# A reordered instruction list for a linear-attention and feed-forward kernel: a lead for each run of small matmuls in the planner's costs

## The chip, the cores and the metric

The kernel runs on one core of a Trainium2 chip. The metric is device time in microseconds. "PE" is TensorE's matmul stream and "PEld" its weight loads, "DVE" is VectorE, "ACT" ScalarE, "POOL" GpSimd, "SP" the engine that issues the DMAs.

## The reference

Four batches of four heads have 1088 positions of 32 dimensions. Queries and keys go through a feature map of 64 products, then linear attention, then a feed-forward layer with a gate over all 4352 tokens:

```python
def phi(x):                        # r = 8
    a = einsum('rd,bhsd->bhsr', S1, x)
    b = einsum('rd,bhsd->bhsr', S2, x)
    return einsum('bhsi,bhsj->bhsij', a, b).reshape(..., 64)
kv  = einsum('bhsf,bhsd->bhfd', phi(k), v)
z   = sum(phi(k), axis=2)
x   = einsum('bhsf,bhfd->bhsd', phi(q), kv) / (einsum('bhsf,bhf->bhs', phi(q), z) + 1e-6)
h   = x @ w_in                     # (4352, 128) @ (128, 2048)
g   = h * clip(h + 3, 0, 6) / 6
out = g @ w_out                    # (4352, 2048) @ (2048, 128)
```

## The kernel before

The tokens are cut into eight chunks of 512 and a last one of 256 that holds what is left over of each batch. A step of the feed-forward part is one chunk and one pair of 128-wide blocks of the hidden layer: six matmuls make h in PSUM (high and low parts of x and w_in, lines 811, 812 and 817), ACT takes relu (825), DVE the gate (828), ACT the high part gh (832), DVE or POOL the low part gl (836), and six matmuls add into o (857, 858 with gh, 860 with gl). There are 8.5 chunks x 8 pairs x 12 = 816 such matmuls of 512 columns, some of them cut into halves of 256.

Ahead of that stand the small operations of the attention part. "ab" projects keys or queries on S1 and S2 (530, and 535 for chunks 2 on, the "far" form), ACT or DVE copies it (539, 543), DVE or POOL makes the products (558), "kv" adds a tile of 128 keys into a batch's PSUM bank (593; ACT copies the finished bank to SBUF at 618), "tr" and "xt" are transposes (713, 664), and "nd" gives numerator and denominator for two tiles of queries (636), which DVE divides (643 to 647). For chunks 2 on, features and x are turned by DVE and through DRAM instead (745, 773, 751, 756, 778, 782). The weights are split into high and low parts in nine passes on ACT and DVE (371 to 396). Loads start at line 423; the first thirteen are chained by a one-element copy on POOL (428), so that one starts after the fourth one before it has landed. Up to 17 us in the plan PE runs a filler matmul (354) where nothing else is ready.

Every engine works through its instructions in the order in which they were emitted, and that order is the plan's. `Plan.order` plays the program through with a cost for each operation: at each point in time it walks the operations whose inputs and buffers are there, least due first, and gives each to an idle engine. The dues come from the constants at the top: STEP between feed-forward steps, DUES for the four stages after h, LAG for o, LEADS for the small operations (a lead is taken off the due; the first set is for batch 0 and chunk 0, the second for the other batches and the far chunks, the third for chunk 1), W_DUE and CONV_LEAD for the weights. gl, the products and some others may go on DVE or POOL; `choose` decides. PSUM has two buffers of two banks for h, two banks "o" and two banks "a" for the small operations; SBUF has 5 buffers for g and 4 each for gh and gl.

Of the kernel before, what the change touches and what calls it, by code (L numbers as in the profile page):

```python
# [23 lines left out]
HP = P // 2  # L24
Q = P // 4
# [24 lines left out]
NEAR = 2  # L50
# [46 lines left out]
SPLIT = 2  # L97


STEP = 5.06  # L100
DUES = (317.92, 316.34, 129.31, 384.08)
LAG = 128.57
W_DUE = (-152.92, 321.22, 23.24, 201.42, 251.62, 14.82, 266.57, 276.24)
CONV_LEAD = (-252.29, -232.94, 463.37, -221.73, 549.89, 31.5, 265.14, 219.73, 219.47)
LOAD_DUE = {}
LEADS = ({'ab': -466.98, 'cp': -244.73, 'ph': 113.36, 'kv': -102.29, 'kvb': -199.83, 'tr': -78.56, 'trcp': -30.35, 'nd': -572.11, 'norm': 297.56, 'xt': 543.02, 'xh': -868.0, 'xl': 204.57, 'k0': -407.3, 'kld': 146.8, 'vld': -256.29, 'qld': -79.85, 'rd': -154.99, 'xw': 402.82, 'xr': 513.46}, {'ab': 106.42, 'cp': 408.81, 'ph': 46.58, 'kv': 85.72, 'kvb': -43.81, 'tr': -441.07, 'trcp': -288.36, 'nd': -2.3, 'norm': -121.67, 'xt': 347.83, 'xh': 86.64, 'xl': 378.1, 'k0': 9.14, 'kld': 371.66, 'vld': 59.77, 'qld': 218.44, 'rd': 139.58, 'xw': 405.77, 'xr': 51.94}, {'ab': -161.26, 'cp': -355.61, 'ph': 225.14, 'kv': -82.13, 'kvb': 258.9, 'tr': -84.99, 'trcp': -282.18, 'nd': 9.09, 'norm': 441.52, 'xt': -380.46, 'xh': -96.54, 'xl': -168.68, 'k0': 149.54, 'kld': -6.91, 'vld': 496.37, 'qld': 447.25, 'rd': -88.95, 'xw': -359.0, 'xr': 167.27})


HOLD = 10.14
HOLD_DUE = -34.33  # L110
SOON = 0.51
SOON_DUE = 27.65
PATIENCE = 0.0


@dataclass(eq=False)
class Op:

# [15 lines left out]
    dual: bool = False  # L134
    moved: float = 0.0
    recs: int = 0


@dataclass(eq=False)
# [9 lines left out]
class Plan:  # L149
# [2 lines left out]
    def __init__(self):  # L152
        self.ops = []

    def add(self, cost, due, deps, emit, bufs=(), cols=0, ready=0.0, moved=0.0, dual=False, recs=0):
        deps = [d for d in deps if d is not None]
        op = Op(cost, due, emit, list(bufs), cols, len(deps), ready, dual=dual, moved=moved, recs=recs)
        for d in deps:
            d.then.append(op)
        for b in op.bufs:  # L160
            b.left += 1
        self.ops.append(op)
        return op

    def fetched(self, t, recs):

        self.begun += recs
        need = self.begun - HELD
        if need > 0:
            t = max(t, self.asked[(need - 1) // MORE] + FETCH)  # L170
        while self.begun >= ASK + MORE * len(self.asked):
            self.asked.append(t)
        return t

    def speed(self, tick):

# [40 lines left out]
    def order(self):  # L217
        self.cols = {}
        self.port = 0.0
        self.begun, self.asked = 0, []  # L220
        self.moving = MOVING
        free, at = dict(BUFS), dict(START)
        free["o"] -= 1
        avail = sorted((o for o in self.ops if not o.waits), key=lambda o: o.due)
        out, ends, wakes, t, left = [], [], [FILL_UNTIL, *at.values()], 0.0, len(self.ops)
        heapify(wakes)
        n_out = 0
        while left:
            t = heappop(wakes)
            while wakes and wakes[0] <= t + 1e-6:  # L230
                t = heappop(wakes)
            t += 1e-7
# [12 lines left out]
            began = []  # L245
            for op in avail:
                if op.ready > t or not all(b.held or any(free[g] for g in b.tags) for b in op.bufs):
                    continue
                e = self.choose(op, t, at, soon)
                if e is None:  # L250
                    continue
                if e == PE and t < FILL_UNTIL and self.short(t, op.cost[PE], op.cols):
                    break
                for b in op.bufs:
                    if not b.held:
                        b.held = True
                        b.tag = next(g for g in b.tags if free[g])
                        free[b.tag] -= 1
                op.engine, op.start = e, t
                op.end = at[e] = self.run(self.fetched(t, op.recs), op.cost[e], op.cols) if e == PE else t + op.cost[e]  # L260
                if e == DVE and op.dual:
                    self.port = op.end
                if e == SP:
                    self.moving = max(self.moving, op.end - ISSUE + BEGUN) + op.moved / RATE
                    op.lat = self.moving + LANDED - op.end
                began.append(op)
            for op in began:
                avail.remove(op)
                n_out += 1
                left -= 1  # L270
                heappush(ends, (op.end + op.lat + FREED, n_out, op))
                heappush(wakes, op.end)
                heappush(wakes, op.end + op.lat + FREED)
                for o in op.then:
                    same = len(o.cost) == 1 and op.engine in o.cost
                    o.ready = max(o.ready, op.end + op.lat + (LATENCY[op.engine] if not same or op.lat else 0.13 if op.engine == DVE else 0.0))
                    o.waits -= 1
                    if not o.waits:
                        insort(avail, o, key=lambda x: x.due)
                        heappush(wakes, o.ready)  # L280
# [45 lines left out]
def fused_kernel(ctx: ExitStack, tc: tile.TileContext, qT, kT, v1, sb, w_in, w_out, outT):  # L326
# [18 lines left out]
    kvb = []  # L345
# [171 lines left out]
    def features(src, n, name, tag, due, ld, srcb, psb, eng_cost, LEAD, far=False, w=HP):  # L517
# [40 lines left out]
            engines[e].tensor_tensor(out, a_, b_, op=ALU.mult)  # L558

        if far:  # L560
            o1 = plan.add({PE: 0.1 + 0.121 * n}, due - LEAD["ab"], [ld], mm_far, [srcb, pb, abb], 256 * n, S_READY, recs=8)
            o2 = plan.add({DVE: 0.12 + 0.067 * n}, due - LEAD["cp"], [o1], cp_far, [pb, abb])
        else:
            o1 = plan.add({PE: 0.13 + 0.115 * n if w == HP else 0.137 + 0.112 * n}, due - LEAD["ab"], [ld], mm, [srcb, pb, abb], 256 * n, S_READY, recs=8 * n if w == HP else 16 * n)
            o2 = plan.add({ACT: 0.06 + 0.0535 * n}, due - LEAD["cp"], [o1], cp, [pb, abb])
        parts = []
        for t0 in range(0, n, SPLIT):
# [9 lines left out]
    def keys(b, due, psbs, ph_eng):  # L577
# [25 lines left out]
        for half in range(2):  # L603
            t0, n = KGROUPS[2 * b + half]
            g = 2 * b + half
            d = due - (LEAD["k0"] if half == 0 else 0)
            lk, kb, kbox = load_keys(g, d - LEAD["kld"])
            lv, vb, vbox = load_values(g, d - LEAD["vld"])
            T, o3, phb = features(kbox, n, f"k{g}", "kph", d, lk, kb, psbs[half], ph_eng[half], LEAD, w=KEY_COLS[b])
            for t in range(n):  # L610
                i = t0 + t - b * KT
                prev = plan.add({PE: 0.175 if KV_COLS[b] == Q else 0.26}, d - LEAD["kv"] + 0.3 * t, [o3[t], lv, prev], partial(kv, t=t, i=i, T=T, vbox=vbox), [phb, vb, kvbuf], 528, recs=32 if KV_COLS[b] == Q else 16)

        def halves(_):
            for e in (0, F):
# [8 lines left out]
    def divided(c, due, T, t, m, ready, phTb, nb, xb, LEAD):  # L624
# [22 lines left out]
            nc.vector.tensor_tensor(x, nd[:, :, 0:D], rden.broadcast_to([P, 4 * m, D]), op=ALU.mult)  # L647

        batches = range(batch_of(c0), batch_of(c0 + n - 1) + 1)
        a = plan.add({PE: 0.1 + 0.26 * m if c < NEAR else 0.11 + 0.245 * m}, due - LEAD["nd"] - lag, [ready, *(o for b in batches for o in kv_done[b])], nd, [phTb, nb, xb], 528 * m, recs=16 * m if c < NEAR else 32 * m)  # L650
        return plan.add({DVE: 0.56 + 0.1 * m}, due - LEAD["norm"] - lag, [a], norm, [nb, xb])

    def turn_x(c, due, T, norms, xb, xpb, LEAD):
# [292 lines left out]
```

## Time and profile before

| what | value |
|---|---|
| median of 3 runs | 246.84 us (245.31 to 247.11) |
| profiled execution, its own time | 244.85 us |
| span of that execution | 243.0 us |
| PE, DVE, ACT, POOL busy | 96%, 76%, 68%, 63% |

The span runs from the first to the last instruction of the profiled execution; 1.85 us of its own time lie around it. Starts in the rows are microseconds from the start of the span. PE's recorded matmuls overlap one another, so the time that one takes is read from start to start.

### The profile page before, as it was taken

Reading aid. Unit: us, or ns where it says so; the run is one execution under the profiler, and the core shown is the slowest. Engines: PE = TensorE matmul, PEld = TensorE weight load, DVE = VectorE, ACT = ScalarE, POOL = GpSimd, SP = SyncE. Lnnn points to the kernel's source line nnn. Section 1 sums busy time; section 2 is a strip of 40 time slices with the busy share of each in tenths; the row PEclk is TensorE's granted clock in tenths of the full one; section 3 lists DMA queues with packets and bytes.
Section 4 is the critical chain, followed back from the end, with each engine's and each line's share of the span. In section 5 each row is a group of like instructions: output and inputs, shape, how many; then the busy total and the mean of one; then the engine's idle time right before and its main releaser. Section 6 shows DMA issues by size and latency. Waiting matters only on the chain.

```text
span 243.0 us, 5464 instructions
## 1 busy us (share of the span) xinstructions
PE 233.8 (96%) x2214; PEld 182.2 (75%) x2214; DVE 184.7 (76%) x246; ACT 164.5 (68%) x205; POOL 154.1 (63%) x102
## 2 busy tenths in 40 slices
PE   8969789999999999999999899999999999999994
PEld 3757666787777778877878687777888878888894
DVE  2869999999899899788657756857648883747643
ACT  3455476888697648756766866849857875878571
POOL 2742867999699998474879844035663305867441
PEclk9999999999999999999999999999999999999999
DMA  6889973032037559704423000000100010001010
GB/s 206 263 282 386 373 249 115 1 88 87 4 87 184 180 146 295 239 0 136 127 89 86 18 29 20 25 0 3 43 0 0 0 43 3 0 0 46 0 43 22
DMA packets 18007, 23.80 MB, mean 98 GB/s; under 512 B 1728, under 2 KB 11072, under 8 KB 17984
## 3 DMA queue, kind: packets, MB, share of 16 engines
q1 hardware_dynamic: 17984, 23.48, 30.5%
q8 instruction: 17, 0.28, 0.5%
q14 instruction: 6, 0.05, 0.1%
HBM read 16.26 MB, written 7.21 MB: 97 GB/s over the span
## 4 chain that ended last, share of the span: by engine, by line
PE 86%; POOL 5%; issue 2%; DMA 2%; ACT 2%; DVE 1%; POOLq 0%; ACTq 0%
PE h L811 13%; PE o L857 13%; PE o L860 13%; PE h L817 12%; PE h L812 12%; PE o L858 12%; PE nd L636 3%; DMA woraw<-w_out_dram 2%; POOL gl L836 2%; PE warm L354 2%; PE kvps L593 2%; POOL ph_k L558 2%; PE abps_k L530 2%; PE abps_q L535 1%; PE xps L664 1%
## 5 line engine op out<-in xcount | busy, mean ns | idle before, releaser
L836 POOL TENSOR_TENSOR gl<-g,gh 128x1024 fp32r<-128x1024 f32 (+1 forms) x50 | 117.9, 2368 | 63.0 <-ACT gh L832 36.9
L828 DVE SCALAR_TENSOR_TENSOR g<-g,h 128x1024 f32<-128x1024 f32 (+1 forms) x72 | 82.9, 1156 | 24.7 <-ACT g L825 24.1
L825 ACT ACTIVATE g<-h 128x1024 f32<-128x1024 f32 (+1 forms) x72 | 70.3, 979 | 40.7 <-POOL gl L836 20.9
L832 ACT CAST gh<-g 128x1024 fp32r<-128x1024 f32 (+1 forms) x72 | 71.5, 1001 | 15.0 <-PE o L858 10.6
L811 PE MATMUL h<-xh,wi_hi 128*128 128x512 f32 (+1 forms) x148 | 56.8, 384 | 0.9 <-DVE g L828 0.9
L817 PE MATMUL h<-xl,wi_hi 128*128 128x512 f32 (+1 forms) x148 | 56.0, 378 | 0.0
L812 PE MATMUL h<-xh,wi_lo 128*128 128x512 f32 (+1 forms) x148 | 55.7, 376 | 0.0
L857 PE MATMUL o<-gh,wo_hi 128*128 128x512 f32 (+1 forms) x144 | 55.6, 389 | 0.0
L858 PE MATMUL o<-gh,wo_lo 128*128 128x512 f32 (+1 forms) x144 | 54.6, 382 | 0.0
L860 PE MATMUL o<-gl,wo_hi 128*128 128x512 f32 (+1 forms) x144 | 43.4, 385 | 0.0
L836 DVE TENSOR_TENSOR gl<-g,gh 128x1024 fp32r<-128x1024 f32 (+1 forms) x22 | 31.6, 1438 | 14.6 <-PE o L860 8.5
L811 PEld LDWEIGHTS h<-xh,wi_hi 128*128 128x128 f32 x148 | 27.7, 187 | 8.5 <-DVE g L828 1.3
L817 PEld LDWEIGHTS h<-xl,wi_hi 128*128 128x128 f32 x148 | 27.7, 187 | 5.9
L857 PEld LDWEIGHTS o<-gh,wo_hi 128*128 128x128 f32 x144 | 27.0, 188 | 6.7 <-issue 0.6
L812 PEld LDWEIGHTS h<-xh,wi_lo 128*128 128x128 f32 x148 | 27.8, 188 | 5.2
L858 PEld LDWEIGHTS o<-gh,wo_lo 128*128 128x128 f32 x144 | 27.0, 188 | 5.4
L860 PEld LDWEIGHTS o<-gl,wo_hi 128*128 128x128 f32 x144 | 25.8, 188 | 5.7 <-issue 0.4
L558 POOL TENSOR_TENSOR ph_k<-ab_k 128x512 f32<-128x512 f32 (+1 forms) x14 | 13.4, 978 | 10.9 <-ACT ab_k L539 10.9
L558 POOL TENSOR_TENSOR ph_q<-ab_q 128x512 f32<-128x512 f32 x15 | 15.8, 1073 | 0.9 <-ACT ab_q L539 0.5
L636 PEld LDWEIGHTS nd<-kvb,phT 128*32 128x32 f32 (+1 forms) x480 | 8.6, 113 | 4.0 <-issue 3.3
L593 PEld LDWEIGHTS kvps<-v,ph_k 128*32 128x32 f32 (+3 forms) x504 | 7.3, 113 | 5.4 <-issue 3.4
L593 PE MATMUL kvps<-v,ph_k 128*32 128x33 f32 (+3 forms) x504 | 8.8, 202 | 2.1 <-issue 1.6
(77 smaller groups left out, 165.8 us busy)
## 6 DMA issues: line engine op xcount, KB each, us to landing
phd<-pht SPq DMA_DIRECT2D x24, 128.0 KB, 3.9
phT<-phd SPq DMA_DIRECT2D x6, 512.0 KB, 4.4
wiraw<-w_in_dram SPq DMA_DIRECT2D x4, 512.0 KB, 5.5
qT<-qT_dram SPq DMA_DIRECT2D x8, 256.0 KB, 5.5
woraw<-w_out_dram SPq DMA_DIRECT2D x4, 512.0 KB, 5.4
outT_dram<-os SPq DMA_DIRECT2D x8, 256.0 KB, 2.0
xd<-xt SPq DMA_DIRECT2D x24, 64.0 KB, 1.8
xT<-xd SPq DMA_DIRECT2D x6, 256.0 KB, 2.7
```

Of the source, the lines that this page charges most:

```text
L558: engines[e].tensor_tensor(out, a_, b_, op=ALU.mult)
L593: nc.tensor.matmul(K["ps"][e : e + k, w], T["ph"][:rows, t, h * F + f : h * F + f + k], vbox[0][:rows, t, w], start=i == 0 and h < 2, stop ...
L811: nc.tensor.matmul(T["h"][:, u, i:j_], wi_hi[:, f], x, start=True, stop=False)
L812: nc.tensor.matmul(T["h"][:, u, i:j_], wi_lo[:, f], x, start=False, stop=False)
L817: nc.tensor.matmul(T["h"][:, u, i:j_], wi_hi[:, f], x, start=False, stop=True)
L825: nc.scalar.activation(T["g"][:, :, :n], T["h"][:, :, :n], AF.Relu, bias=3.0, scale=1.0)
L828: nc.vector.scalar_tensor_tensor(T["g"][:, :, :n], T["g"][:, :, :n], 6.0, T["h"][:, :, :n], op0=ALU.min, op1=ALU.mult)
L832: nc.scalar.copy(T["gh"][:, :, :n], T["g"][:, :, :n])
L836: engines[e].tensor_tensor(T["gl"][:, :, :n], T["g"][:, :, :n], T["gh"][:, :, :n].bitcast(F32), op=ALU.subtract)
L857: nc.tensor.matmul(o, wo_hi[:, f], T["gh"][:, u, :n], start=first and u == 0, stop=False)
L858: nc.tensor.matmul(o, wo_lo[:, f], T["gh"][:, u, :n], start=False, stop=False)
L860: nc.tensor.matmul(o, wo_hi[:, f], T["gl"][:, u, :n], start=False, stop=last and u == 1)
```

## The change

Two things change. First, the cost of a small operation on PE is split in two: a cost for itself, and a lead that the plan adds when the operation just before it on PE was of another kind. Kinds are "ab", "far", "kv" and "nd"; all other operations have no kind and no lead, and they end a run. The cost of an operation that stands alone stays within 0.03 us of what it was, but for kv in the batch-0 form (0.26 to 0.36 us) and in the other form (0.175 to 0.26 us). What the operations emit is untouched.

Second, all constants that set the order have new values. In LEADS, the second set has for example nd from -2.3 to -47.89, kld from 371.66 to 610.73 and qld from 218.44 to 355.87. `choose` itself is as before, so its rule for gl and the products is changed through SOON, SOON_DUE and PATIENCE alone, and its rule for holding an engine free through HOLD and HOLD_DUE.

```diff
-STEP = 5.06
-DUES = (317.92, 316.34, 129.31, 384.08)
-LAG = 128.57
-W_DUE = (-152.92, 321.22, 23.24, 201.42, 251.62, 14.82, 266.57, 276.24)
-CONV_LEAD = (-252.29, -232.94, 463.37, -221.73, 549.89, 31.5, 265.14, 219.73, 219.47)
+STEP = 4.31
+DUES = (334.45, 304.68, 247.67, 421.33)
+LAG = 116.65
+W_DUE = (-66.68, 326.64, -31.04, 253.22, 362.18, -253.11, 299.63, 339.63)
+CONV_LEAD = (-304.42, -129.34, 469.79, -119.14, 763.88, 26.11, 358.72, 292.57, 281.21)
...
-HOLD = 10.14
-HOLD_DUE = -34.33
-SOON = 0.51
-SOON_DUE = 27.65
-PATIENCE = 0.0
+HOLD = 33.3
+HOLD_DUE = -86.68
+SOON = 6.01
+SOON_DUE = -49.92
+PATIENCE = 0.93
...
+    def taken(self, op):
+
+        cost = op.cost[PE] + (op.lead if op.kind != self.last else 0.0)
+        self.last = op.kind
+        return cost
...
-                op.end = at[e] = self.run(self.fetched(t, op.recs), op.cost[e], op.cols) if e == PE else t + op.cost[e]
+                op.end = at[e] = self.run(self.fetched(t, op.recs), self.taken(op), op.cols) if e == PE else t + op.cost[e]
...
                 op = Op({PE: 0.214}, 0.0, self.filler, [], 512, start=t, engine=PE, recs=2)
+                self.last = ""
...
-            o1 = plan.add({PE: 0.1 + 0.121 * n}, due - LEAD["ab"], [ld], mm_far, [srcb, pb, abb], 256 * n, S_READY, recs=8)
+            o1 = plan.add({PE: 0.107 * n}, due - LEAD["ab"], [ld], mm_far, [srcb, pb, abb], 256 * n, S_READY, recs=8, lead=0.156, kind="far")
...
-            o1 = plan.add({PE: 0.13 + 0.115 * n if w == HP else 0.137 + 0.112 * n}, due - LEAD["ab"], [ld], mm, [srcb, pb, abb], 256 * n, S_READY, recs=8 * n if w == HP else 16 * n)
+            o1 = plan.add({PE: 0.115 * n if w == HP else 0.112 * n}, due - LEAD["ab"], [ld], mm, [srcb, pb, abb], 256 * n, S_READY, recs=8 * n if w == HP else 16 * n, lead=0.135, kind="ab")
...
-                prev = plan.add({PE: 0.175 if KV_COLS[b] == Q else 0.26}, d - LEAD["kv"] + 0.3 * t, [o3[t], lv, prev], partial(kv, t=t, i=i, T=T, vbox=vbox), [phb, vb, kvbuf], 528, recs=32 if KV_COLS[b] == Q else 16)
+                prev = plan.add({PE: 0.15 if KV_COLS[b] == Q else 0.25}, d - LEAD["kv"] + 0.3 * t, [o3[t], lv, prev], partial(kv, t=t, i=i, T=T, vbox=vbox), [phb, vb, kvbuf], 528, recs=32 if KV_COLS[b] == Q else 16, lead=0.11, kind="kv")
...
-        a = plan.add({PE: 0.1 + 0.26 * m if c < NEAR else 0.11 + 0.245 * m}, due - LEAD["nd"] - lag, [ready, *(o for b in batches for o in kv_done[b])], nd, [phTb, nb, xb], 528 * m, recs=16 * m if c < NEAR else 32 * m)
+        a = plan.add({PE: 0.25 * m if c < NEAR else 0.233 * m}, due - LEAD["nd"] - lag, [ready, *(o for b in batches for o in kv_done[b])], nd, [phTb, nb, xb], 528 * m, recs=16 * m if c < NEAR else 32 * m, lead=0.135, kind="nd")
```

## Rows read from the trace of the kernel before

**Rows 1.** The page of the profile: the span, and the busy time of PE and DVE.

```profile
span 243.0 us, 5464 instructions
...
PE 233.8 (96%) x2214; PEld 182.2 (75%) x2214; DVE 184.7 (76%) x246; ACT 164.5 (68%) x205; POOL 154.1 (63%) x102
```

**Rows 2.** The view of the span by stretches: length, busy time of each engine (instructions), granted clock, DMA share, GB/s. The first six rows cut the span at the events told in the text, the last one is the stretch from 40 to 80 us.

```profile
0.00:5.55 5.55, 4.78 (x11) 1.46 (x11) 1.25 (x7) 1.93 (x4) 1.49 (x11) 1.00 0.59 190
5.55:33.40 27.85, 23.51 (x623) 18.52 (x622) 23.84 (x47) 13.83 (x29) 15.03 (x23) 1.00 0.92 322
33.40:134.85 101.45, 101.45 (x1060) 77.27 (x1060) 88.81 (x130) 73.79 (x87) 85.78 (x46) 1.00 0.41 118
134.85:135.75 0.90, 0.05 (x2) 0.01 (x1) 0.84 (x1) 0.90 (x2) 0.88 (x1) 1.00 0.00 0
135.75:239.81 104.06, 104.06 (x522) 84.96 (x522) 69.98 (x63) 73.69 (x84) 50.95 (x23) 1.00 0.04 16
239.81:243.00 3.19, 0.00 (x1) 0.00 (x0) 0.00 (x0) 0.38 (x1) 0.00 (x0) 0.85 0.12 41
...
40.00:80.00 40.00, 40.00 (x434) 30.28 (x433) 38.87 (x56) 31.68 (x39) 36.65 (x21) 1.00 0.33 88
```

**Rows 3.** PE in order of time, a stretch of feed-forward steps without a small operation (48 matmuls from the first row to the second).

```profile
46.94 0.40 PE L857 MATMUL o<-gh,wo_hi 128*128 128x512 f32 x1
...
58.14 0.40 PE L811 MATMUL h<-xh,wi_hi 128*128 128x512 f32 x1
```

**Rows 4.** PE in order of time around visits to small operations: the last big matmul before, the small ones, and the first two big ones after.

```profile
59.31 0.40 PE L817 MATMUL h<-xl,wi_hi 128*128 128x512 f32 x1
...
59.64 0.77 PE L593 MATMUL kvps<-v,ph_k 128*32 128x33 f32 x64
...
60.33 0.50 PE L857 MATMUL o<-gh,wo_hi 128*128 128x512 f32 x1
...
60.67 0.39 PE L858 MATMUL o<-gh,wo_lo 128*128 128x512 f32 x1
...
61.46 0.67 PE L636 MATMUL nd<-kvb,phT 128*32 128x66 f32 x32
...
62.06 0.50 PE L860 MATMUL o<-gl,wo_hi 128*128 128x512 f32 x1
...
82.09 1.13 PE L636 MATMUL nd<-kvb,phT 128*32 128x66 f32 x64
83.16 0.50 PE L857 MATMUL o<-gh,wo_hi 128*128 128x512 f32 x1
...
33.40 0.33 PE L593 MATMUL kvps<-v,ph_k 128*32 128x33 f32 x16
33.73 0.47 PE L811 MATMUL h<-xh,wi_hi 128*128 128x512 f32 x1
```

**Rows 5.** PE in order of time: the first and the last visit to small operations after 33.73 us (19 in all), and the last nd run of the far chunks (10 runs for 13 operations; the first is the one at 61.46 us in Rows 4).

```profile
35.30 0.89 PE L593 MATMUL kvps<-v,ph_k 128*32 128x33 f32 x64
...
168.69 0.67 PE L636 MATMUL nd<-kvb,phT 128*32 128x66 f32 x32
...
171.72 0.38 PE L664 MATMUL xps<-ident,x 128*128 128x128 f32 x2
```

**Rows 6.** PE in order of time in the ramp: where it stood idle, with the idle time and its releaser in brackets, and the first and the last of the five fillers there (x2 is two).

```profile
6.59 0.39 PE L354 MATMUL warm<-const-bfloat16-1.0 128*128 128x512 bf16 x1
...
15.18 0.65 PE L530 MATMUL abps_k<-s_ab,kT 128*32 128x64 f32 x32 [1.80 <-ACT mag_wo L371]
...
17.34 0.60 PE L354 MATMUL warm<-const-bfloat16-1.0 128*128 128x512 bf16 x2
...
24.99 0.76 PE L593 MATMUL kvps<-v,ph_k 128*32 128x33 f32 x64 [0.42 <-POOL ph_k L558]
...
27.40 0.25 PE L593 MATMUL kvps<-v,ph_k 64*32 64x33 f32 x4 [0.82 <-issue]
...
32.29 0.45 PE L593 MATMUL kvps<-v,ph_k 128*32 128x33 f32 x29 [0.74 <-issue]
```

**Rows 7.** ACT and POOL in order of time around that first hole.

```profile
14.44 0.66 ACT L371 ACTIVATE mag_wo<-woraw 128x512 f32<-128x512 f32 x1 [2.03 <-DMA woraw<-w_out_dram]
15.00 0.42 ACT L618 COPY kvb<-kvps 64x66 f32<-64x66 f32 x2
...
15.17 0.18 POOL L428 COPY qT<-kT 128x1 f32<-128x1 f32 x1 [0.45 <-DMA kT<-kT_dram]
```

**Rows 8.** The one hole of PE after the ramp, and POOL before it.

```profile
127.61 8.12 POOL L836 TENSOR_TENSOR gl<-g,gh 128x1024 fp32r<-128x1024 f32 x3
...
135.75 0.50 PE L811 MATMUL h<-xh,wi_hi 128*128 128x512 f32 x1 [0.85 <-DVE g L828]
```

**Rows 9.** The groups of gl on the page: where it ran, its duration, and what POOL idled for.

```profile
L836 POOL TENSOR_TENSOR gl<-g,gh 128x1024 fp32r<-128x1024 f32 (+1 forms) x50 | 117.9, 2368 | 63.0 <-ACT gh L832 36.9
...
L836 DVE TENSOR_TENSOR gl<-g,gh 128x1024 fp32r<-128x1024 f32 (+1 forms) x22 | 31.6, 1438 | 14.6 <-PE o L860 8.5
```

**Rows 10.** gl alone on DVE and POOL from 40 to 80 us: busy time (instructions).

```profile
40.00:80.00 40.00, 0.00 (x0) 26.27 (x11) 1.00 0.33 88
```

**Rows 11.** The end of the span: the last matmuls, the last copy.

```profile
239.42 0.39 PE L860 MATMUL o<-gl,wo_hi 128*128 128x256 f32 x2
...
239.85 0.38 ACT L876 ACTIVATE os<-o 128x256 f32<-128x256 f32 x1 [2.40 <-PE o L860]
```

More of the change, by code (lines that the diff above doesn't have):

```diff
@@ L97 @@
 SPLIT = 2
-STEP = 5.06
-DUES = (317.92, 316.34, 129.31, 384.08)
-LAG = 128.57
-W_DUE = (-152.92, 321.22, 23.24, 201.42, 251.62, 14.82, 266.57, 276.24)
-CONV_LEAD = (-252.29, -232.94, 463.37, -221.73, 549.89, 31.5, 265.14, 219.73, 219.47)
-LOAD_DUE = {}
-LEADS = ({'ab': -466.98, 'cp': -244.73, 'ph': 113.36, 'kv': -102.29, 'kvb': -199.83, 'tr': -78.56, 'trcp': -30.35, 'nd': -572.11, 'norm': 297.56, 'xt': 543.02, 'xh': -868.0, 'xl': 204.57, 'k0': -407.3, 'kld': 146.8, 'vld': -256.29, 'qld': -79.85, 'rd': -154.99, 'xw': 402.82, 'xr': 513.46}, {'ab': 106.42, 'cp': 408.81, 'ph': 46.58, 'kv': 85.72, 'kvb': -43.81, 'tr': -441.07, 'trcp': -288.36, 'nd': -2.3, 'norm': -121.67, 'xt': 347.83, 'xh': 86.64, 'xl': 378.1, 'k0': 9.14, 'kld': 371.66, 'vld': 59.77, 'qld': 218.44, 'rd': 139.58, 'xw': 405.77, 'xr': 51.94}, {'ab': -161.26, 'cp': -355.61, 'ph': 225.14, 'kv': -82.13, 'kvb': 258.9, 'tr': -84.99, 'trcp': -282.18, 'nd': 9.09, 'norm': 441.52, 'xt': -380.46, 'xh': -96.54, 'xl': -168.68, 'k0': 149.54, 'kld': -6.91, 'vld': 496.37, 'qld': 447.25, 'rd': -88.95, 'xw': -359.0, 'xr': 167.27})
-HOLD = 10.14
-HOLD_DUE = -34.33
-SOON = 0.51
-SOON_DUE = 27.65
-PATIENCE = 0.0
+STEP = 4.31
[3 more added lines that the diff above has]
+CONV_LEAD = (-304.42, -129.34, 469.79, -119.14, 763.88, 26.11, 358.72, 292.57, 281.21)
+LOAD_DUE = {}
+LEADS = ({'ab': -412.15, 'cp': -326.18, 'ph': 97.12, 'kv': 2.11, 'kvb': -467.32, 'tr': 2.94, 'trcp': -199.99, 'nd': -493.05, 'norm': 300.27, 'xt': 562.42, 'xh': -826.62, 'xl': 273.94, 'k0': -388.4, 'kld': 185.32, 'vld': -260.13, 'qld': 153.85, 'rd': -347.91, 'xw': 515.91, 'xr': 488.45}, {'ab': 101.81, 'cp': 447.08, 'ph': -75.15, 'kv': 72.05, 'kvb': 108.18, 'tr': -403.05, 'trcp': -266.36, 'nd': -47.89, 'norm': -170.28, 'xt': 328.11, 'xh': -122.6, 'xl': 393.0, 'k0': 24.53, 'kld': 610.73, 'vld': -71.26, 'qld': 355.87, 'rd': 29.1, 'xw': 220.04, 'xr': 54.17}, {'ab': -116.77, 'cp': -474.19, 'ph': 283.03, 'kv': -24.83, 'kvb': 337.37, 'tr': -48.73, 'trcp': -260.0, 'nd': 5.34, 'norm': 345.01, 'xt': -503.62, 'xh': -321.35, 'xl': -246.99, 'k0': 30.86, 'kld': -194.6, 'vld': 436.55, 'qld': 598.55, 'rd': -94.74, 'xw': -529.34, 'xr': 129.65})
+HOLD = 33.3
[3 more added lines that the diff above has]
+PATIENCE = 0.93
 @dataclass(eq=False)
@@ L136 @@
     recs: int = 0
+    lead: float = 0.0
+    kind: str = ""
 @dataclass(eq=False)
@@ L153, in __init__, with add @@
         self.ops = []
-    def add(self, cost, due, deps, emit, bufs=(), cols=0, ready=0.0, moved=0.0, dual=False, recs=0):
+    def add(self, cost, due, deps, emit, bufs=(), cols=0, ready=0.0, moved=0.0, dual=False, recs=0, lead=0.0, kind=""):
         deps = [d for d in deps if d is not None]
-        op = Op(cost, due, emit, list(bufs), cols, len(deps), ready, dual=dual, moved=moved, recs=recs)
+        op = Op(cost, due, emit, list(bufs), cols, len(deps), ready, dual=dual, moved=moved, recs=recs, lead=lead, kind=kind)
         for d in deps:
@@ L219, in order @@
         self.port = 0.0
-        self.begun, self.asked = 0, []
+        self.begun, self.asked, self.last = 0, [], ""
         self.moving = MOVING
```

## The prediction

> **What bounds the kernel now.** I read the page first: PE is busy for 233.8 of 243.0 us and DVE for 184.7 [rows 1]. So the end is set by how much PE has to do and by where it stands idle, and the view by stretches says where that is [rows 2]. Five stretches: until 5.55 us PE has only fillers; from 5.55 to 33.40 us (the ramp) it works 23.51 of 27.85 us, 4.34 us idle, with the DMA engines at 0.92; from 33.40 to 239.81 us it has one single hole, 0.85 us before 135.75 us; the last 3.19 us are the copy out and the store of the last chunk. The granted clock is full (1.00) in every stretch in which PE works, so there's nothing to win or lose there.
>
> Inside the dense part a big matmul takes 11.20 us / 48 = 0.2333 us from start to start [rows 3]. 816 of them are 190.4 us, the same in either list. What an order can change is the rest: 243.0 - 190.4 = 52.6 us, of which 5.55 us are the fixed start, 3.19 us the tail, 4.34 + 0.85 us holes, about 1.8 us the five fillers in the ramp (0.39 us for one, 0.60 us for two, [rows 6]); the remaining 36.9 us are the small operations with everything that a visit to them costs.
>
> **What a visit to small operations costs.** In order of time, PE goes from the last big matmul at 59.31 us to kv at 59.64 us: 0.33 us where 0.23 us is usual, so 0.10 us to enter. Behind the visit the first big matmul takes 60.67 - 60.33 = 0.34 us, so 0.11 us to leave. One nd operation (32 recorded matmuls) takes 62.06 - 61.46 = 0.60 us, two joined 83.16 - 82.09 = 1.07 us; the second one costs 0.47 us, so a lone one pays 0.13 us of its own [rows 4]. A visit thus costs 0.10 + 0.11 + 0.13 = 0.34 us beyond the work, and a join of two visits gives 0.34 us back. For kv it is the like: one operation alone took 33.73 - 33.40 = 0.33 us, four joined 60.33 - 59.64 = 0.69 us [rows 4], 0.12 us for each further one and 0.21 us of lead. I use 0.34 us for every kind; for the far form no joined pair exists in the trace, so for it this is an estimate from nd.
>
> The Trainium skill (page TensorE: Matmul & The Clock Gate, section Back-to-back issue gap) gives small matmuls a floor of some 25 ns from start to start, whatever their size. By that 32 of them take 0.8 us in any company, a run is bound by its count, and joining would be worth nothing in itself. The second nd operation of the pair took 0.47 us / 32 = 14.7 ns each, so the trace does not bear that floor out here, and I go by the rows.
>
> **The change part by part.**
>
> Joins. After 33.73 us there are 19 visits, 10 of them nd runs for 13 operations [rows 4, 5]. The rule that picks an operation does not look at kinds; the lead only prices a run, and the constants decide whether like operations come to be ready together. The bounds: nd in pairs throughout would save 3 visits, and far, ab and kv next to their like perhaps 3 more, 6 x 0.34 = 2.0 us gained; the three nd pairs and one kv four that exist could be split, 4 x 0.34 = 1.4 us lost. I take 3 joins, -1.0 us, because three of ten nd runs are pairs without any price on it, so a second operation isn't far from ready. A join makes the first operation later; its cover is the x of the next chunk, which is turned through DRAM well ahead.
>
> The ramp. Its bounds are wide: all idle time and all fillers gone would be -6.1 us, and the four holes (1.80, 0.42, 0.82 and 0.74 us, [rows 6]) once more would be +3.8 us. The largest has a clear cause: ACT's copy of the first kv bank at 15.00 us stood behind the first pass on w_out, which waited until 14.44 us for its load, and PE's own next load (keys) landed only by 15.17 us, when POOL's one-element copy that waits for it could start [rows 7]. By their dues the copy of kv (199.83 before, 467.32 after) is ahead of that pass (503.91 before, 666.60 after) in both lists, so it was the plan's idea of when each would be ready that put them so, and its figures for loads are the same after. I expect this hole to stay. The other three are 0.42 to 0.82 us each, and I let one of them go: -0.5 us. New positions of the loads for later batches (kld and qld, on SP's queue and past POOL's copies) count here too: at 0.92 DMA share an earlier one is paid by the weights.
>
> The hole at 135 us. POOL took three gl in a row from 127.61 us, 8.12 us, the buffers of g filled, and relu and gate came late by 0.85 us [rows 8]. PATIENCE and SOON move gl between POOL (2.37 us) and DVE (1.44 us, [rows 9]). Bounds: the hole goes, -0.85 us; two more like it come, +1.7 us. I take half of it, -0.4 us.
>
> The tail. o of the last chunk ends the list in both; its last matmul starts at 239.42 us, the copy at 239.85 us [rows 11], and nothing in the diff shortens the 3.19 us behind. 0 us.
>
> Sum: -1.0 - 0.5 - 0.4 = -1.9 us. Against the profiled execution, 244.85 us, that is 242.95 us (a span of 241.1 us). The median of the three runs lies 1.99 us above that execution; on it the forecast is 246.84 - 1.9 = 244.9 us.
>
> **The rivals.**
>
> The ramp closes. If the new order gets the kv copy ahead of the waiting pass, the 1.80 us hole goes and some of the fillers with it, 2.5 us more than the sum: 242.4 us. For it: nothing but an order holds the copy back, since kv itself was done before. Against it: DVE is busy for 23.84 us of the 27.85 us of the ramp and for 38.87 of 40 us from 40 to 80 us [rows 2], so PE may be ahead at 33 us and wait for DVE at 60 us.
>
> Gl goes over to DVE where DVE is full (slower). With PATIENCE at 0.93 the plan keeps gl for DVE if DVE comes free within 0.93 x 2.35 - 1.137 = 1.05 us; at 0 it never waited. From 40 to 80 us all 11 gl run on POOL [rows 10], and DVE has 40 - 38.87 = 1.13 us left. One gl there (1.44 us) already overruns that; four are 5.8 us, 4.6 us too many, and behind them in DVE's queue stand the gates, which free h, and the weight passes. Less the 1.4 us from joins and the later hole, that is +3.2 us, 250.0 us. It decides from the second gl moved in this stretch. Against it: the larger SOON sends gl to POOL whenever a more urgent operation of DVE is known for the next 6 to 8 us.
>
> The list prices joins and none come about: since the rule of choice is blind to kinds, as many visits as before, and the other terms cancel: 246.5 us.
>
> **How the numbers follow.** What tells from no change here is 1%, 2.5 us: under 244.4 us is faster, over 249.3 us slower. The forecast (243.2 to 246.6 us, its own range) has 0.45, of it 0.10 under 244.4 us and 0.02 for a loss that the bounds allow; the closing ramp 0.27; gl on DVE 0.18; no joins 0.10, of it 0.01 slower. So faster 0.37, same 0.42 (0.33 + 0.09), slower 0.21. The range goes from 241.5 us (past the closing ramp, with half of the second bound of the joins) to 249.0 us (into the gl case); that leaves about 0.07 below and 0.12 above.
>
> **What would show it.** In the profile after: visits to small operations after the ramp counted from PE's order of time, 16 instead of 19, the longer nd runs near 1.07 us; PE's idle time from 5.55 us to the first dense stretch, 3.8 us instead of 4.3; no hole over 0.5 us behind it; gl from 40 to 80 us still on POOL. I'm wrong if the idle time of the ramp moves by more than 1.5 us either way, if PE has several holes between 40 and 140 us behind gates (gl on DVE), or if the count of visits rises.

## The result, and the profile after

The changed kernel took 247.57 us (median of 19 runs, 246.18 to 248.82), the kernel before 245.53 us beside it (19 runs): a ratio of 1.008, 95% interval 1.0056 to 1.0103. A gain of 1.9 us was forecast, a loss of 2.0 us came: within 1% and inside the range, but on the other side.

The first reading is the page of the changed kernel: the span, the busy times and the two groups of gl. Its line numbers are 10 above those of before (L846 is the L836 of [rows 9]).

```profile
span 246.3 us, 5439 instructions
...
PE 235.2 (96%) x2217; PEld 182.6 (74%) x2217; DVE 198.8 (81%) x264; ACT 163.9 (67%) x205; POOL 121.5 (49%) x84
...
L846 POOL TENSOR_TENSOR gl<-g,gh 128x1024 fp32r<-128x1024 f32 x37 | 90.5, 2449 | 81.7 <-ACT g L835 31.2
...
L846 DVE TENSOR_TENSOR gl<-g,gh 128x1024 fp32r<-128x1024 f32 (+1 forms) x35 | 40.7, 1174 | 4.4 <-ACT gh L842 3.8
```

The span is 3.3 us longer than in [rows 1]. PE's busy time grew by 1.4 us, DVE's by 14.1 us (184.7 to 198.8), and POOL's fell by 32.6 us (154.1 on the page of before). gl moved: DVE now has 35, before 22 [rows 9].

The second is the view by stretches, with the columns of [rows 2]; the 33.40:37.10 and the 40:80 (gl alone, on PE, PEld, DVE and POOL) are cut out of the same view.

```profile
5.55:33.40 27.85, 22.98 (x522) 17.69 (x522) 25.02 (x48) 13.56 (x28) 14.71 (x21) 1.00 0.90 299
33.40:134.85 101.45, 99.24 (x1039) 74.97 (x1031) 92.10 (x121) 71.23 (x85) 66.60 (x38) 0.98 0.37 109
...
243.05:246.30 3.25, 0.00 (x0) 0.00 (x0) 0.00 (x0) 0.38 (x1) 0.00 (x0) 1.00 0.11 40
...
33.40:37.10 3.70, 3.70 (x24) 2.29 (x16) 2.28 (x5) 2.90 (x5) 3.67 (x4) 0.56 0.82 246
...
40.00:80.00 40.00, 6.48 (x20) 3.60 (x20) 0.00 (x0) 25.56 (x11) 1.00 0.33 93
```

PE's idle time in the ramp is 27.85 - 22.98 = 4.87 us (4.34 before), in the dense part 101.45 - 99.24 = 2.21 us (0.85 before, all of it in the one hole). The tail is 3.25 us (3.19). And from 33.40 to 37.10 us the granted clock is 0.56, so mostly the lower level (1.2 GHz), where before had 1.00 in this place. From 40 to 80 us all 11 gl are still on POOL, as in [rows 10].

The third is PE in order of time: every hole over 0.5 us after 13 us, what ran before the longest, two big matmuls of the stretch with the low clock, and the first and last visit to small operations after 33.8 us.

```profile
16.91 0.44 PE L674 MATMUL xps<-ident,x 128*128 128x128 f32 x2 [1.13 <-ACT xh L691]
...
20.84 0.69 PE L646 MATMUL nd<-kvb,phT 128*64 128x66 f32 x16 [0.68 <-ACT phT L729]
...
26.70 0.49 PE L821 MATMUL h<-xh,wi_hi 128*128 128x512 f32 x1 [0.78 <-ACT xh L691]
...
27.35 0.77 PE L603 MATMUL kvps<-v,ph_k 128*32 128x33 f32 x64
28.05 0.65 PE L545 MATMUL abps_q<-qT,s_sb 128*64 128x256 f32 x4
28.63 0.68 PE L603 MATMUL kvps<-v,ph_k 128*32 128x33 f32 x55
31.31 0.54 PE L603 MATMUL kvps<-v,ph_k 128*32 128x33 f32 x25 [2.00 <-issue]
...
35.30 0.63 PE L822 MATMUL h<-xh,wi_lo 128*128 128x512 f32 x1
35.73 0.63 PE L827 MATMUL h<-xl,wi_hi 128*128 128x512 f32 x1
...
39.51 0.77 PE L540 MATMUL abps_k<-s_ab,kT 128*32 128x64 f32 x40
...
86.61 0.50 PE L827 MATMUL h<-xl,wi_hi 128*128 128x512 f32 x1 [1.00 <-DVE xl L695]
...
106.43 0.50 PE L821 MATMUL h<-xh,wi_hi 128*128 128x512 f32 x1 [0.99 <-DVE g L838]
...
200.69 0.38 PE L674 MATMUL xps<-ident,x 128*128 128x128 f32 x2
```

Four things are to be seen. The hole of 1.80 us behind ACT's pass [rows 6] is gone. A new one of 2.00 us stands inside a kv run: nothing but "issue" released it, and 55 + 25 matmuls are five operations of 16, of which three and seven matmuls of the fourth had run, so no data can be missing. Two of the dense part, 1.00 and 0.99 us, follow an xl and a gate of DVE. And big matmuls start 35.73 - 35.30 = 0.43 us apart at the low clock, against 0.233 us in [rows 3].

Where the 3.3 us of the profiled span came from:

| term | forecast | measured |
|---|---|---|
| visits to small operations, 19 to 18 | -1.0 (to 16) | -0.3 (1 x 0.34) |
| idle time of the ramp | -0.5 | +0.5 |
| holes of the dense part | -0.4 | +1.4 |
| tail | 0 | +0.1 |
| granted clock, 3.70 us x (1 - 0.56) | 0 | +1.6 |
| sum | -1.9 | +3.3 |

The clock doesn't explain the ratio, though. 11 of the 19 runs of the changed kernel have a mean granted clock of 0.993 (mean span 246.2 us) and 8 have 1.00 (244.8 us). The kernel before has such runs too: 27 of the 63 that stood beside all later runs were below 0.996, and the 36 others have a mean span of 242.8 us. At the full clock the two kernels are thus 2.0 us apart, as their medians are. Without the clock the table gives +1.7 us; 0.3 us are not placed. The larger part of it, 1.4 us, are the holes of the dense part. The +0.5 us of the ramp are a difference of sums: the stops by "issue" are 2.00 us where the two of [rows 6] were 1.56 us, and the waits for data 1.13 + 0.68 + 0.78 = 2.59 us where they were 2.43 us (1.80, 0.42 and one of 0.21 us at 7.18 us).

### The profile page after: what moved, and what is told of

Read it like the earlier page. It is cut to its first block, busy times and chain, and to the rows that moved or that the text cites. A ratio compares the mean times of both kernels' runs of the same rounds, so it can differ in the third digit from the quotient of the medians.

```text
span 246.3 us, 5439 instructions
## 1 busy us (share of the span) xinstructions
PE 235.2 (96%) x2217; PEld 182.6 (74%) x2217; DVE 198.8 (81%) x264; ACT 163.9 (67%) x205; POOL 121.5 (49%) x84
## 4 chain that ended last, share of the span: by engine, by line
PE 81%; DVE 9%; issue 3%; DMA 2%; ACT 2%; POOL 1%; DVEq 0%; ACTq 0%
PE h L821 12%; PE o L867 12%; PE h L827 12%; PE o L870 12%; PE h L822 11%; PE o L868 11%; PE nd L646 3%; DVE g L838 3%; DMA wiraw<-w_in_dram 2%; PE kvps L603 2%; PE warm L364 2%; PE abps_k L540 2%; DVE xl L695 2%; PE abps_q L545 2%; DVE pht L755 1%
## 5 line engine op out<-in xcount | busy, mean ns | idle before, releaser
L846 POOL TENSOR_TENSOR gl<-g,gh 128x1024 fp32r<-128x1024 f32 x37 | 90.5, 2449 | 81.7 <-ACT g L835 31.2
L846 DVE TENSOR_TENSOR gl<-g,gh 128x1024 fp32r<-128x1024 f32 (+1 forms) x35 | 40.7, 1174 | 4.4 <-ACT gh L842 3.8
L568 POOL TENSOR_TENSOR ph_k<-ab_k 128x512 f32<-128x512 f32 (+1 forms) x12 | 11.8, 1000 | 12.3 <-ACT ab_k L549 12.1
L646 PE MATMUL nd<-kvb,phT 128*32 128x66 f32 (+1 forms) x480 | 10.2, 223 | 0.7 <-ACT phT L729 0.7
```

What stands on the lines that cost most here:

```text
L646: nc.tensor.matmul(W["nd"][e : e + w, o : o + 2 * DV], T["phT"][:, p, i : i + w], kvb[batch_of(c0 + i)][:, p, :], start=True, stop=True)
L846: engines[e].tensor_tensor(T["gl"][:, :, :n], T["g"][:, :, :n], T["gh"][:, :, :n].bitcast(F32), op=ALU.subtract)
```

## What the experiments told apart

The first question was what stops PE inside the kv run. Theory F: PE runs out of instructions, because a run of small matmuls uses them up faster than they come. Its rival: something else of that place (data, the queue order) holds it. The second was what stands behind the two dense holes. Theory P: a DVE operation with two operands in SBUF stands still while POOL works. Theory L, the mechanism of my slower rival: DVE has too much to do. In the edits below, seq is the order that the plan gives, a list of operations, and the numbers are places in it.

**Five kv operations of the run later, behind four big matmuls (kv_later).**

```diff
+    late, at = [seq[i] for i in (169, 173, 175, 177, 178, 183)], seq[185]
+    seq = [o for o in seq if o not in late]
+    n = seq.index(at) + 1
+    seq[n:n] = late
```

(The sixth one is ACT's copy of their bank. The expectation counts six big matmuls; in the trace four, 1.1 us in all, now stand between the two kv runs.)

> The list of the changed kernel, with five kv operations (the run of 80 at 28.6 us, in the midst of which PE stood for 2.00 us) and the copy of their bank moved behind the next six big matmuls. Theory F (PE runs out of fetched instructions: two kv runs and a far one take 246 instructions in 2 us, and the next block comes 2.6 us after its transfer starts): the six big matmuls take 1.4 us with 12 instructions and cover the fetch, the hole shrinks from 2.00 to under 0.6 us, the clock stays at full in the 33 to 37 us stretch (granted 1.00 instead of 0.56), and the time falls by 1.4 to 2.9 us against the changed kernel, to a ratio of 0.996 to 1.003 to the kernel before. Theory D (kv waits for its products or values): the operation is as late as before, the hole stays at some 0.6 to 1.4 us after the move or goes into the next wait, and what is gained is the 1.4 us of cover alone, with the place of the stop at the start of an operation and not inside one.

Measured: 245.72 us (10 runs), ratio to before 1.0048 (1.0031 to 1.0066). What PE waited for, in total, times, longest:

```profile
PE h L821 <- DVE g L838: 1.4, 2, 1.0
PE h L827 <- DVE xl L695: 1.0, 1, 1.0
...
PE kvps L603 <- issue: 0.6, 1, 0.6
```

The stop fell from 2.00 to 0.60 us, and it is still inside a run (after 51 of the 80 matmuls that were moved). So the stop follows the run of small matmuls, and it is shorter with big ones ahead of that run: F. The length varies from run to run: in the traces of the four kernels of this document with kv moved it is 0.59 to 1.20 us, in the five with the same narrow matmuls where they were it is 1.46 to 2.00 us. The ratio missed the 0.996 to 1.003 that F had let me expect. All ten runs have a mean clock of 0.998 or more; at that clock the mean span is 244.0 us, 0.8 us under the changed kernel's, where the hole alone would give 1.4 us. Part of the difference is seen: a second hole behind a gate, 0.4 us (1.4 us in two, 1.0 the longest).

**The same kv work with wider matmuls (kv_wide).** KV_COLS sets how many columns of the array one matmul of kv takes (32 or 64); with 64 throughout 288 of them are recorded in place of 504. The plan's costs stay, so the order does too.

```diff
-            k = KV_COLS[b]
+            k = HP
```

> The list of the changed kernel, with the kv matmuls of batches 1 to 3 emitted 64 wide instead of 32 wide: the same work in half the instructions, each operation longer by some 0.1 us. Theory F: the hole inside kv at 29 to 31 us goes from 2.00 us to under 0.6 us, though nothing of the data came earlier. Theory D: a hole of 1.5 to 2 us stays there. The time: kv takes 27 x 0.1 = 2.7 us more, less the hole, so about as the changed kernel or 1 us more.

Measured: 247.34 us, one run, clock 1.00. PE in order of time:

```profile
27.29 1.13 PE L603 MATMUL kvps<-v,ph_k 128*64 128x33 f32 x32
28.25 0.63 PE L545 MATMUL abps_q<-qT,s_sb 128*64 128x256 f32 x4
28.71 1.43 PE L603 MATMUL kvps<-v,ph_k 128*64 128x33 f32 x40
```

The same list with fewer instructions has no stop at all, at the same place and with the same data: F again. It isn't a cure: four kv operations take 28.25 - 27.29 = 0.96 us in place of 28.05 - 27.35 = 0.70 us, and the dense holes stay.

**Instructions come in blocks.** The trace also holds the transfers of the queue of instructions, 16 KB each. Around the stops, in us:

```
kernel          transfer starts    PE resumes    its stop
before          25.09              27.40         0.82 (kv)
before          29.76              32.29         0.74 (kv)
changed         28.68              31.31         2.00 (kv)
```

Each stop ends 2.3 to 2.6 us after a block's transfer starts. The same holds for every such stop of this document: the 15 stops of 0.4 us or more, in 13 traces, end 2.2 to 2.8 us after the start of a transfer of 16 KB. From 27.35 to 29.31 us PE used up 64 + 4 + 55 = 123 matmuls and as many weight loads, 246 instructions in 2.0 us. So the two "issue" rows of [rows 6] were the same thing.

The Trainium skill (page Runtime: NRT & Kernel Launch, section Instruction fetch mechanics) says that blocks of 16 KiB are fetched ahead and that the fetch is hidden, since instructions are issued more slowly than they come. The size agrees with the trace; that it is hidden does not, with stops of 0.5 to 2.2 us in these runs.

**Two DVE operations on POOL, the xl before the first dense hole and the ph_q before the second (xl_pool).** First DVE and POOL of the changed kernel in order of time (start, duration):

```profile
83.71 2.85 DVE L695 TENSOR_TENSOR xl<-xT,xh 128x512 fp32r<-128x512 f32 x1
...
99.98 0.72 DVE L695 TENSOR_TENSOR xl<-xT,xh 128x512 fp32r<-128x512 f32 x1
100.62 2.89 DVE L568 TENSOR_TENSOR ph_q<-ab_q 128x512 f32<-128x512 f32 x1
...
83.61 2.40 POOL L846 TENSOR_TENSOR gl<-g,gh 128x1024 fp32r<-128x1024 f32 x1 [2.76 <-ACT gh L842]
...
97.74 5.23 POOL L846 TENSOR_TENSOR gl<-g,gh 128x1024 fp32r<-128x1024 f32 x2 [0.38 <-ACT gh L842]
```

The xl at 83.71 us took 2.85 us, the next one 0.72 us. It ended at 86.56 us, 0.55 us after POOL's gl, which had started 0.10 us before it. ph_q ended 0.54 us after the second gl of POOL's pair, and that pair took 5.23 us where two single ones take 4.8 us. So each of the two DVE operations stood until POOL was done, and the pair's length fits one of its gl having waited for the xl at 99.98 us.

The Trainium skill (page SBUF — State Buffer, section Who interferes with whom) has this rule: a DVE instruction with both inputs in SBUF and a GpSimd instruction that reads SBUF share a port pair, and the second to start waits for the whole of the first. These rows agree, and so do the next two kernels.

```diff
+    for i in (449, 524):
+        seq[i].engine = POOL
```

> The list of the changed kernel, with the low part of x at 83.7 us and one product of queries at 100.6 us on POOL in place of DVE, each at its place in the list. Theory P (a DVE operation with two SBUF inputs stands while POOL works: 2.85 us instead of 0.7, twice): both collisions go, the two holes of PE of 1.00 us at 86.6 and 0.99 us at 106.4 us go with them, time falls by 1.5 to 2.2 us, ratio to before 0.998 to 1.003. Theory L (DVE has simply too much to do since 35 instead of 22 gl are on it): 1.3 us less work on DVE, the holes shrink by about that in sum. Rival N: the holes come back later in the dense part and the time stays at 1.008.

Measured: 244.74 us (10 runs), ratio 1.0007 (0.9977 to 1.0038). PE's waits:

```profile
PE kvps L603 <- issue: 1.6, 1, 1.6
PE abps_k L540 <- DMA kT<-kT_dram: 0.9, 1, 0.9
PE h L821 <- ACT xh L691: 0.8, 1, 0.8
```

No wait of the dense part is left; the kv stop is 1.57 us in this run, and at the full clock (5 runs) the mean span is 242.2 us, 2.6 us under the changed kernel's. The dense holes are 2.2 us of that; the other 0.4 us are within what the waits of the ramp differ by from run to run.

**The colliding gl on DVE instead (gl_dve).** xl_pool relieves DVE and ends the collision in one; this one ends the collision and loads DVE further.

```diff
+    for i in (461, 533):
+        seq[i].engine = DVE
```

> The list of the changed kernel, with the two gl on POOL that stood across those two DVE operations moved to DVE, so DVE has 37 gl. Theory P: two collisions of 2.2 us each go, 2 x 1.15 us of work come, the holes at 86.6 and 106.4 us shrink by over half, and the time falls by 1 to 2 us (ratio 0.999 to 1.005). Theory L (DVE's load is the cause): the holes grow by up to 2.3 us in sum and the time rises to 1.010 to 1.018.

Measured: 245.08 us (10 runs), ratio 1.0013 (0.9974 to 1.0051). The two operations of DVE that had stood:

```profile
82.58 0.69 DVE L695 TENSOR_TENSOR xl<-xT,xh 128x512 fp32r<-128x512 f32 x1
...
98.41 0.68 DVE L568 TENSOR_TENSOR ph_q<-ab_q 128x512 f32<-128x512 f32 x1
```

And the one wait of PE that is left in the dense part:

```profile
PE h L821 <- DVE g L838: 0.5, 1, 0.5
```

With two more gl DVE is quicker at both places: 0.69 and 0.68 us, and 0.5 us of holes remain of 2.2 us. P holds, L falls.

**Both repairs, and a third.** "Both" is the two POOL operations and the later kv; "three" also puts ACT's pass that waited for its load until 15.94 us (mag_wi, ahead of xh and of the hole at 16.91 us) further back:

```diff
+    for i in (449, 524):
+        seq[i].engine = POOL
+    late, at = [seq[i] for i in (169, 173, 175, 177, 178, 183)], seq[185]
...
+    late, at = [orig[i] for i in (87,)], orig[104]
```

> The list of the changed kernel with both edits at once: five kv operations behind the next six big matmuls, and the low part of x and the product on POOL. If the hole in the ramp (with the clock after it) and the two collisions in the dense part are separate causes, their gains add: kv_later's 245.7 us less the 2.0 us of dense holes, 243.7 us, ratio 0.993 to 0.999 to the kernel before. If one of them only moves a wait that the other would have met anyway, the time stays at 244.7 us or above (ratio about 1.000).

> As the kernel with both edits, and in addition the first pass of the second w_in block on ACT (it stood until 15.8 us for its load, with the copies for the first chunk queued behind it) moved behind those copies. If the 1.13 us hole of PE at 16.9 us is due to that queue, it goes, and 0.8 to 1.1 us more are gained (242.7 us, ratio 0.989 to 0.995). Rival: the weight pass itself is then late, or DVE, which works 25.0 of 27.85 us in the ramp, takes the place; then the time equals that of both edits.

Measured: 243.87 us, ratio 0.9965 (0.9938 to 0.9992), and 243.47 us, ratio 0.9923 (0.9885 to 0.9961), 10 runs each. Both are faster than either kernel, against the kernel before by 0.4 and 0.8%. Two of the waits of "three":

```profile
PE xps L674 <- DVE x L657: 1.2, 1, 1.2
PE kvps L603 <- issue: 1.2, 1, 1.2
```

The third edit did not take its hole away: xps waits 1.2 us for DVE's x where it waited for ACT, and "both" without that edit has 1.1 us there, also behind x. So it isn't told apart from "both". Besides, that hole is not a fixed one: in kernels whose lists agree with the changed one up to that point, the waits of PE from 15 to 18 us are 0.3 (kv_wide) to 1.8 us (nd_split) in sum, 1.1 us in the changed kernel, so a single trace doesn't price it. At the full clock "both" is only 0.2 us under xl_pool (242.0 and 242.2 us); what the later kv adds to it is above all that all 20 runs of these two kept the clock, against 5 of 10.

**One half of the change at a time.** The new costs and leads with the old constants (costs_only):

```diff
-STEP = 4.31
+STEP = 5.06
...
-PATIENCE = 0.93
+PATIENCE = 0.0
```

> The kernel before with the new costs and leads, and the old constants: only the first part of the change. The theory that the price of a run makes the plan join like operations: visits to small operations after the ramp fall from 19 to 16 or fewer, time falls by 1 us (ratio 0.994 to 0.998). The theory that the lead is blind, because the choice doesn't look at kinds: visits stay at 18 to 20, the order drifts where it may, and the time is anywhere within 1% either way, more likely slower, as constants searched for one set of costs meet another (ratio 1.000 to 1.012).

And the new constants in the kernel before, with its costs (constants_only):

```diff
-STEP = 5.06
+STEP = 4.31
...
-PATIENCE = 0.0
+PATIENCE = 0.93
```

> The kernel before with its old costs, and the new constants: only the second part of the change. If the constants carry what happened (fewer of gl on POOL, the tight kv runs, the collisions), DVE has 30 to 38 gl as in the changed kernel, and the time is slower than before by 0.3 to 1.5%. If instead the slowdown comes from the leads, the time is within 0.4% of before.

Measured: 258.99 us (4 runs), ratio 1.0551 (1.0451 to 1.0652), and 258.11 us (4 runs), ratio 1.0547 (1.0421 to 1.0673). The longest waits of each:

```profile
PE h L821 <- ACT xh L691: 2.5, 1, 2.5
PE abps_q L545 <- issue: 2.2, 1, 2.2
```

```profile
PE h L811 <- DVE g L828: 5.8, 5, 2.2
PE abps_k L530 <- DVE wi_lo L396: 2.4, 1, 2.4
```

Both came out far beyond what was expected, 1.012 and 1.015 at most. Neither half can be priced alone: parting the constants from the costs that they were chosen with costs 13 to 14 us against the kernel before either way, part of it clock (a mean of 0.96 to 0.987 in all eight runs). Two things can be read from the traces even so. With the new costs alone the visits rise to 21, and DVE has 23 gl; the price of a run does not by itself make the plan join anything. With the new constants alone DVE has 32 gl: the constants moved them.

**A small nudge of one lead.** 0.005 us less for nd (nudge), and 0.006 us less for far (nudge2), all else as in the changed kernel:

```diff
-... lead=0.135, kind="nd")
+... lead=0.13, kind="nd")
```

```diff
-... lead=0.156, kind="far")
+... lead=0.15, kind="far")
```

> The changed kernel with one number of the plan's costs changed: the lead of nd is 0.130 instead of 0.135 us, all constants as they are; the list is worked out anew and differs from the changed one in some 80 places, and the plan's own end is 0.08 us later. If time follows from the leads as such, nothing happens: ratio 1.006 to 1.010. If it hangs on where single operations come to lie (a collision here, a run there), the ratio moves by more than its interval, anywhere from 0.995 to 1.02, though nothing that one would call a change was made.

> The same with the lead of the far form, 0.150 instead of 0.156 us; the list differs in some 250 places and the plan's own end is 2.0 us later. If time follows from the leads, nothing (247 to 248 us); if it hangs on the places of single operations, 2 us or more later (249 us or above), in step with the plan's end.

Measured: 246.97 us (10 runs), ratio 1.0065 (1.0029 to 1.0102), and 252.60 us (one run). The first is another list of the same quality, with its holes elsewhere (2.5 us in two behind xl, 1.7 us "issue"); its ratio is one that was expected if nothing changes. The second lost 5 us in its one run:

```profile
PE h L821 <- DVE g L838: 5.5, 3, 2.1
PE kvps L603 <- issue: 1.5, 1, 1.5
```

What the plan itself reckoned for the landing of the last store, in us, beside the time measured:

```
                     plan     measured
before               235.9    245.5
changed              236.0    247.6
nd lead 0.130        236.1    247.0
far lead 0.150       238.0    252.6
costs only           244.5    259.0
constants only       248.4    258.1
```

The plan sees a large loss, and not one of 2 us; the time measured is 9.6 to 14.6 us above its own. It isn't that it lacks the two causes above. `fetched` (in the diff of the change) lets PE go on only when it reckons the block of instructions to have come, and `choose` starts no DVE operation that the plan marks as having two inputs in SBUF (gl, products of far chunks, the later xl) while POOL works, and nothing on POOL while such an operation runs on DVE. The two terms gave the wrong answer. In the changed list the plan has one wait for instructions, 0.23 us at 26.68 us, where 2.00 us were measured (in the list before five, 1.24 us in sum). And it ends the xl at 78.16 us, 1.80 us before that gl of POOL starts, and the ph_q 1.14 us before its gl. In the trace DVE reached the xl 6.16 us behind the plan and POOL the gl only 3.65 us behind it, so they met. The list fixes the order on each engine, and nothing in it makes POOL's gl wait for DVE's xl.

**Four joined nd pairs parted (nd_split).** "Both" with the second nd operation of four pairs moved behind a later operation of PE (orig is the order as the plan gave it):

```diff
+    late, at = [orig[i] for i in (467,)], orig[469]
+    seq = [o for o in seq if o not in late]
+    n = seq.index(at) + 1
+    seq[n:n] = late
+    late, at = [orig[i] for i in (633,)], orig[634]
...
+    late, at = [orig[i] for i in (727,)], orig[728]
...
+    late, at = [orig[i] for i in (818,)], orig[821]
```

> The kernel with both edits, and four of its joined pairs of nd split again: the second operation of each pair behind the next o group (two or four big matmuls), three of them past 120 us, where PE has no idle time. By the price read from the rows of before (0.34 us for a visit), four visits more cost 1.4 us: 245.2 us, ratio 1.000 to 1.004 to the kernel before, and a pair that took 1.07 us becomes two runs of 0.60 us with entries and exits of 0.33 us on either side. By the leads of the changed list alone (0.135 us each) they cost 0.5 us, 244.4 us. By a fixed floor for each small matmul, whatever its company, they cost nothing, 243.9 us.

Measured: 245.54 us (10 runs), ratio 1.0005 (0.9964 to 1.0047); 1.67 us above "both" by the medians, 1.5 us by the mean spans at the full clock (243.6 and 242.0 us). One of the parted pairs on PE:

```profile
85.88 0.39 PE L827 MATMUL h<-xl,wi_hi 128*128 128x512 f32 x1
86.20 0.67 PE L646 MATMUL nd<-kvb,phT 128*32 128x66 f32 x32
86.80 0.73 PE L870 MATMUL o<-gl,wo_hi 128*128 128x512 f32 x2
87.47 0.67 PE L646 MATMUL nd<-kvb,phT 128*32 128x66 f32 x32
88.07 0.50 PE L867 MATMUL o<-gh,wo_hi 128*128 128x512 f32 x1
88.41 0.39 PE L868 MATMUL o<-gh,wo_lo 128*128 128x512 f32 x1
```

0.32 us into the visit (0.23 usual), 0.60 us for a lone operation, 0.34 us for the first big matmul behind it: the prices of [rows 4] again, and four visits cost 1.5 to 1.7 us where 4 x 0.34 = 1.4 us was reckoned. The kernel before was 0.5 us slower beside this one (245.41 us) than beside "both" (244.90 us); by the ratios the difference is 1.0 us. So 0.25 to 0.4 us a visit. A part may not be the visits: the stop by "issue", ahead of all four pairs, is 0.88 us in this trace and 0.59 us in that of "both".

**The kernel before with wider kv matmuls (before_wide).**

```diff
-            k = KV_COLS[b]
+            k = HP
```

> The kernel before, its list untouched, with the kv matmuls of batches 1 to 3 emitted 64 wide, half the instructions. If its two holes inside kv runs (0.82 us at 27.4 us and 0.74 us at 32.3 us) are waits for instructions too, both go (under 0.3 us in sum), while kv takes longer by some 0.1 us each. If they are waits for data, they stay at 0.6 to 0.9 us each.

Measured: 246.26 us, one run. PE's waits:

```profile
PE nd L636 <- issue: 1.8, 1, 1.8
...
PE kvps L593 <- POOL ph_k L558: 0.7, 1, 0.7
PE kvps L593 <- DMA v<-v_dram: 0.6, 1, 0.6
PE abps_k L530 <- ACT mag_wo L371: 0.6, 1, 0.6
```

Both stops inside kv are gone, but one of 1.8 us stands inside nd now, at 23.39 us, and kv waits for its data instead, 0.7 and 0.6 us. The transfer of a block starts at 21.19 us here (in the kernel before at 18.71 and 25.09 us), and the nd stands until 2.20 us later. So halving one run can move the stop to another dense run instead of healing it.

The last line is the hole of 1.80 us of [rows 6]: in the same list up to there it is 0.58 us here, because ACT's pass got its load by 12.86 us and not by 14.44 us.

## Why the prediction was wrong, point by point

Joins. The mechanism and the price hold (parting four pairs cost 0.25 to 0.4 us each); the count was mis-sized. nd is joined, 8 runs in place of 10, but the other kinds gave one visit back, so one join of three: -0.3 us in place of -1.0 us. The Trainium skill's floor of some 25 ns from start to start (page TensorE: Matmul & The Clock Gate, section Back-to-back issue gap), by which joining is worth nothing, does not agree with nd_split either.

The ramp. This step failed in two ways. I expected the 1.80 us hole to stay, because both lists have like dues for the kv copy and the pass on w_out. It went; ACT of the changed kernel, in order of time:

```profile
12.38 0.43 ACT L628 COPY kvb<-kvps 64x66 f32<-64x66 f32 x2
12.84 0.68 ACT L381 ACTIVATE mag_wo<-woraw 128x512 f32<-128x512 f32 x1
...
15.94 0.66 ACT L381 ACTIVATE mag_wi<-wiraw 128x512 f32<-128x512 f32 x1 [2.02 <-DMA wiraw<-w_in_dram]
```

The copy now stands 0.46 us ahead of the pass. So like dues in both lists did not tell which of the two comes first: a due decides only among operations that are ready. In the plan of the kernel before, ACT comes free at 11.58 us, 0.02 us before the copy may start, and takes the pass; in the changed one it comes free at 11.81 us, when both may start, and the due decides. The hole's size was in part that of one execution, too (0.58 us in before_wide). And the gain didn't come. Other waits for data took the place of the 1.80 us, 2.59 us in sum where there had been 2.43 us. I took all holes as such waits, of which an order may heal one, and didn't ask what "issue" inside a run of like matmuls in [rows 6] can be, though `fetched` in the diff is a term for just that. It is a limit of its own, and the new order, with its longest kv run closer packed, ran into it for 2.00 us. The bound of +3.8 us held; the value, -0.5 us, was on the wrong side by 1.0 us.

The dense part. The hole before 135.75 us went, as I half expected, and two others of 1.0 us came, inside the bound of +1.7 us. The step that failed is the price of gl and of what runs beside it. [Rows 8] already show it: three gl in 8.12 us are 2.71 us each where a single one takes 2.40 us, and the DVE mean of 1438 ns in [rows 9] mixes undisturbed ones of 1.22 to 1.23 us and halves of 0.69 us with ones that took up to 2.64 us. I took both for plain durations.

The rival "gl goes over to DVE". gl did go over, 13 of them, and PE does have a hole behind a gate and one behind an xl of DVE, but not by that mechanism: none moved between 40 and 80 us, DVE was less busy there (37.54 us of 40 by the view of that stretch, 38.87 before), and gl_dve shows that two more on DVE make it faster. By its sign of recognition I might have called it right; the experiment says otherwise.

The tail: 3.25 us for 3.19 us, as said. The clock: I wrote that nothing was to be lost there. The profiled run lost 1.6 us, but the kernel before loses the like in some of its runs too.

What stays open: what makes the clock fall, and what either half of the change is worth by itself. Long stops and the low clock go together only loosely: none of 30 runs of the three kernels with kv moved and a stop of 0.6 to 1.2 us (kv_later, "both", "three") had a mean clock under 0.996, 11 of the 30 with a stop near 1.6 us (xl_pool, gl_dve, nudge) did, and 11 of the 19 with 2.00 us. But nd_split, with 0.9 us, had it in 2 of 10, and the kernel before, with two of 0.8 and 0.7 us, in 27 of 63. The run of small matmuls before the stop was not tried apart from the stop.

## What to carry to other kernels

A released-by-"issue" gap in the middle of a run of small matmuls was a shortage of instructions here: count the instructions in the microseconds before it, and spread such runs among big matmuls, whose instructions are few. Before a group's mean duration is used as a price, look at its least and greatest: on DVE and POOL a long one was often a wait for the other engine, and who works beside whom is then a matter of the order. A plan may have a term for each of these and still miss the single case, because its times drift from the chip's (6 us at the xl here) and its list orders each engine only in itself. So its own end doesn't rank lists that are 2 us apart, and a small change of its costs can be a new draw (0.006 us in one lead, 5 us in one run); look at the holes of the draw and mend those by hand.

## What the runs showed of the hardware

In the changed kernel PE used up 246 small instructions in 2.0 us. In 13 kernels it stood 0.5 to 2.2 us where the next block of 16 KB came late, and went on 2.2 to 2.8 us after that block's transfer had started. A DVE operation with two inputs in SBUF took 2.85 and 2.89 us in place of 0.68 to 0.72 us beside a gl of POOL, with no wait recorded, only a longer duration.
